# Long convolution and spectral mixing on one core: the last 64 positions of two sequences in one result tile, and the last pair's copies of u on ScalarE

## The chip, the core and the metric

The kernel runs on one core of a Trainium2 chip. The core has TensorE (PE in the profile, its weight loads are PEld), VectorE (DVE), ScalarE (ACT), GpSimd (POOL) and SyncE (SP), which here only issues transfers. Sixteen DMA engines move data between HBM and the on-chip memory SBUF. Matmul results land in PSUM, eight banks of 512 fp32 columns on 128 partitions, from which only DVE and ACT copy here.

The metric is the device time of one execution in microseconds (us). The profile shows one execution instruction by instruction. Its span, from the first to the last instruction, is a little shorter than the time of the same execution.

## What is computed

```python
def _attn_ref(x, h) -> np.ndarray:
    B, S, D = x.shape
    L = 2 * S
    Xf = np.fft.rfft(x, n=L, axis=1)
    Hf = np.fft.rfft(h, n=L, axis=0)
    Yf = Xf * Hf[None, :, :]
    y = np.fft.irfft(Yf, n=L, axis=1)[:, :S, :]
    return y.astype(np.float32)
...
def _moe_ref(x, w_r, w_i, w_ch) -> np.ndarray:
    ...
    X = np.fft.rfft(x, axis=1)
    ...
    Y[:, :n_modes] = Yr + 1j * Yi
    y = np.fft.irfft(Y, n=S, axis=1)
    u = x + y
    return (u + np.maximum(u @ w_ch, 0.0)).astype(np.float32)
```

The input x is 8 sequences of 5696 positions with 128 channels. A long convolution along the positions comes first. Then 64 low modes are mixed across channels, which gives u, and the result is u + relu(u W) at each position, with W of 128x128.

## The kernel before

Everything is worked out as discrete Fourier transforms by matmul, for two sequences at a time: the eight sequences are four pairs, `g_` from 0 to 3, and `b` is the sequence within the pair. Up to about 266 us of the span the spectra of all pairs are made, multiplied by the filter and written to a scratch tensor in HBM. From there on the output phase runs, and all of the change lies in it.

**u tiles.** `u_tile` makes one eighth of u for one sequence: 712 positions, as a 128x712 tile with the channels on the partitions. Its 18 matmuls (two with `IBs` and `C`, sixteen with `S4a` or `S4b` and a spectrum tile `ZT`) fill two PSUM banks. One copy then brings it to SBUF as fp16 in the tensor `UT` (L801, through `evac`, whose line is L311 on ACT and L315 on DVE). A counter decides the engine: of every eight copies five go to ACT and three to DVE (L798). A sequence's u is whole after eight u tiles.

**Result tiles.** `o_tile` makes the results of 512 positions: four matmuls with a slice of `UT` as weights and `WI` (W and the identity, 256 columns) as the moving operand, so that PSUM has u W and u side by side in two banks. ACT makes `R` = relu(u W) (L870), DVE adds u to it (L871) into a buffer `O` or `Os`, and SP sends the buffer to HBM (L320). 5696 positions are 11 such full tiles and 64 positions over; these 64 positions are a twelfth, small tile with one matmul, 64x128 in R and in O, and a transfer of 32 KB. Two full tiles in succession share one `O` buffer and one transfer of 512 KB (the "wide" ones); others have one of 256 KB. There are 7 buffers `O`, 4 buffers `Os`, and 3 buffers `R`.

**Slots.** u tiles and result tiles take PSUM in turn from one ring of four slots of two banks each (`LSLOT`). So the matmuls of a tile wait until the tile four places earlier has been read out: a u tile by its one copy, a result tile by its relu and its add.

**Order.** The order is written out by the loops at L887 to L903, and each engine works through its own list in that order. A list `todo` holds the result tiles still to be made. After each u tile of pair 1 and of pair 2 one or two result tiles of the pair before are taken from it, in turn (24 in all, two sequences with 12 tiles each). In the last pair the u tiles of sequence 0 come first, eight of them, with two result tiles after each; then the eight of sequence 1, with two and three in turn, for which the tiles of the last pair's own sequence 0 have been added to `todo`. The twelve result tiles of the last sequence follow when no u tile is left; this stretch is called the drain here. In the text a step is one u tile with the result tiles that follow it.

The spectrum tiles `ZT` come from the scratch tensor in HBM, in five buffers, by transfers on SP's queue between those of the results.

Of the kernel before, what the change touches and what calls it, by code (L numbers as in the profile page):

```python
# [4 lines left out]
P = 128  # L5
# [118 lines left out]
def bass_long_conv_fft__then__afno_spectral_mix_kernel(nc, x, h, moe_w_r, moe_w_i, moe_w_ch, out):  # L124
    B, S, D = x.shape
# [7 lines left out]
    NP = B // 2  # L133
# [26 lines left out]
    rows = s4.transpose(1, 0, 2, 3).reshape(2 * NK, S)  # L160
# [45 lines left out]
    def at(name, cols, dt, off):  # L206
        return nc.alloc_sbuf_tensor_at(name, [P, cols], dt, offset=off)
# [62 lines left out]
    u_sb = [at(f"UT{i}", S, F16, u_off[i]) for i in range(4)]  # L270
# [21 lines left out]
    def pv(bank, off, dims, p0=0, n=P):  # L292
        return bass.AP(ps, p0 * 4096 + bank * 512 + off, [[4096, n]] + [list(d) for d in dims])
# [5 lines left out]
    def bank(i):  # L299
        return ("bank", i)  # L300
# [3 lines left out]
    def evac(dst, src, reads, writes, scale=None, eng=None, after=()):  # L304
        e = eng
        if e is None:
            turn[0] ^= 1
            e = "scalar" if turn[0] else "vector"
        if e == "scalar":
            if scale is None:  # L310
                R.add(e, lambda h_: h_.copy(dst, src), reads, writes, after=after)  # L311
            else:
                R.add(e, lambda h_: h_.activation(dst, src, COPY, scale=scale), reads, writes, after=after)  # L313
        elif scale is None:
            R.add(e, lambda h_: h_.tensor_copy(dst, src), reads, writes, after=after)  # L315
        else:
            R.add(e, lambda h_: h_.tensor_scalar_mul(dst, src, scale), reads, writes, after=after)  # L317

    def dma(eng, dst, src, ring, reads=(), writes=(), after=()):
        R.add(eng, lambda h_: h_.dma_start(dst, src), reads, writes, ring=ring, after=after)  # L320

    def mm(o, l, r, st, sp, reads, writes):
        R.add("tensor", lambda h_: h_.matmul(o, l, r, start=st, stop=sp), reads, writes)  # L323
# [3 lines left out]
    def once(key, toks):  # L327
        if key in first:
            return []
        first[key] = 1  # L330
        return list(toks)
# [3 lines left out]
    def turns(name, items):  # L335
        i = ring2.get(name, 0)
        ring2[name] = i + 1
        return items[i % len(items)]
# [384 lines left out]
    for g_ in range(NP):  # L723
# [15 lines left out]
        if g_ + 1 < NP:  # L739
            for j in range(6, 32):  # L740
# [3 lines left out]
                if wp and j % 2 == 1:  # L744
                    dst, src_, ring, tok = wp.pop(0)
# [10 lines left out]
    NCH = J // ZB  # L756
    n_ev = [0]
    ahead = {}

    def u_z(i, b, half, alone=False, parts=(0, 1)):  # L760
        g_, c_ = divmod(i, NCH)
        t = ahead.get((i, b, half))
        if t is None:
            t = turns("l", LSLOT)
        z = zt[i % NC]
        for hb in parts:
            if not alone:
                u_c(i, b, half, t, hb, True)
            for pl in range(4):
                for ri in range(2):  # L770
                    pz = half * 8 + hb * 4 + pl
                    so = (c_ * ZB + pz) * NQ
                    n = (P, PB + RB)[ri]
                    mm(pv(t + hb, pl * NQ, [[1, NQ]]), z[ri][0:n, pz * 256 + b * P:pz * 256 + b * P + P], s4_sb[ri][0:n, so:so + NQ],
                       alone and pl == 0 and ri == 0, not alone and pl == 3 and ri == 1, [("zt", i % NC, ri), ("zt0", i % NC), ("s4", ri, 0)] + ([("s4", ri, 1)] if c_ >= NCH // 2 else []), [bank(t + hb)])
        if alone:
            ahead[(i, b, half)] = t
        return t

    def u_c(i, b, half, t, hb, first_):  # L780
        g_, c_ = divmod(i, NCH)
        pl0 = half * 8 + hb * 4
        mm(pv(t + hb, 0, [[1, 4 * NQ]]), c_sb[:, (2 * g_ + b) * P:(2 * g_ + b + 1) * P],
           ib_sb[:, (c_ * ZB + pl0) * NQ:(c_ * ZB + pl0 + 4) * NQ], first_, not first_,
           [("c", g_ // 2), ("ib", 0)] + ([("ib", 1)] if c_ >= NCH // 2 else []), [bank(t + hb)])

    def u_tile(i, b, half):
        g_, c_ = divmod(i, NCH)
        t = ahead.get((i, b, half))
        if t is None:  # L790
            t = u_z(i, b, half)
        else:
            for hb in range(2):
                u_c(i, b, half, t, hb, False)
        ub = (g_ % 2) * 2 + b
        old = {0: WT, 1: WT, 2: U_ALL, 3: U_ALL}[ub]
        n_ev[0] += 1
        e = "scalar" if n_ev[0] % 8 in (0, 2, 3, 5, 7) else "vector"  # L798
        src = pv(t, 0, [[1, NQ], [512, 2], [NQ, 4]])
        evac(bass.AP(u_sb[ub], c_ * ZB + half * 8, [[S, P], [J, NQ], [4, 2], [1, 4]]),  # L800
             src, [bank(t), bank(t + 1)], [("u_", ub, 2 * c_ + half)], eng=e, after=once(("u", ub), old))  # L801
# [36 lines left out]
    NW = S // P  # L838
    TAIL = S - NW * P

    def o_tile(g_, b, r4):
        ub = (g_ % 2) * 2 + b
        bb = 2 * g_ + b
        t = turns("l", LSLOT)
        i = n_o[0]
        n_o[0] += 1
        full = r4 < NW // 4
        last_ = (g_, b) == (NP - 1, 1)
        wide = r4 < (8 if last_ else NW // 4 // 2 * 2)
        big = wide or (last_ and full)  # L850
        h_ = r4 % 2 if wide else 0
        if big:
            if not h_:
                o_cur[0] = turns("o8", list(range(NO8)))
            ob, key, old = o8_sb[o_cur[0]], ("o8", o_cur[0]), o8_old[o_cur[0]]
        else:
            k_ = turns("os", list(range(NO)))
            ob, key, old = o_sb[k_], ("os", k_), o_old[k_]
        OW = 1024 if big else 512
        n, rows = (4, P) if full else (1, TAIL)  # L860
        rd = [("u_", ub, c_) for c_ in range(2 * NCH)] + [("wch",), ("i16",)]
        for j in range(n):
            lh = bass.AP(u_sb[ub], 4 * r4 + j, [[S, P], [NW, P]]) if full else u_sb[ub][:, NW * P:S]
            mm(pv(t + j // 2, (j % 2) * 256, [[1, 256]], 0, rows), lh, WI, True, True, rd, [bank(t + j // 2)])
        bk = [bank(t), bank(t + 1)] if full else [bank(t)]
        rs = r_sb[i % NR]
        rv = bass.AP(rs, 0, [[512, rows], [P, n], [1, P]])
        ov = bass.AP(ob, h_ * 512, [[OW, rows], [P, n], [1, P]])
        src_r, src_u = pv(t, 0, [[256, n], [1, P]], 0, rows), pv(t, P, [[256, n], [1, P]], 0, rows)
        R.add("scalar", lambda e: e.activation(rv, src_r, RELU), bk, [("r", i % NR)], after=once(("r", i % NR), G_ALL + XTT + [("y", 0), ("y", 1), ("id",)]))  # L870
        R.add("vector", lambda e: e.tensor_tensor(ov, src_u, rv, ADD), bk + [("r", i % NR)],  # L871
              [key + (h_,)], after=once(key, old))
        if wide and not h_:
            return
        w_ = (2 if wide else 1) * 4 * D
        if full:
            dst = bass.AP(out.tensor, out.offset + bb * S * D + (4 * r4 - 4 * h_) * D, [[NW * D, P], [1, w_]])
            src = ob[:, 0:w_]
        else:
            dst = bass.AP(out.tensor, out.offset + bb * S * D + NW * P * D, [[D, TAIL], [1, D]])  # L880
            src = ob[0:TAIL, 0:P]
        dma("sync", dst, src, "o", [key + (v_,) for v_ in range(h_ + 1)])

    todo = []
    NB = NCH * NP
    NW4 = NW // 4 + 1
    for g_ in range(NP):  # L887
        last = g_ == NP - 1
        order = [(c_, b) for b in range(2) for c_ in range(NCH)] if last else [(c_, b) for c_ in range(NCH) for b in range(2)]
        for n, (c_, b) in enumerate(order):  # L890
            i = NCH * g_ + c_
            for half in range(2):
                u_tile(i, b, half)
                for _ in range((2, 2 + half)[n >= NCH] if last else 1 + half):
                    if todo:
                        o_tile(*todo.pop(0))
            if b == 1 and i + NC < NB:
                load_zt(i + NC)
            if last and n == NCH - 1:
                todo += [(g_, 0, r4) for r4 in range(NW4)]  # L900
        todo += [(g_, b, r4) for b in range(1 if last else 0, 2) for r4 in range(NW4)]
    while todo:
        o_tile(*todo.pop(0))  # L903
    R.add("sync", lambda e: e.nop(), [], [("o8", i, v_) for i in range(NO8) for v_ in range(2)] + [("os", i, 0) for i in range(NO)])
# [31 lines left out]
```

## Time and profile before

| | |
|---|---|
| time, median of 3 runs | 385.36 us (385.15 to 385.92) |
| the profiled execution: time, span | 385.31 us, 383.2 us |
| busy time in the span: PE, DVE, ACT, POOL | 360.0, 303.1, 310.7, 84.4 us |
| matmuls | 5346 |
| copies of u on ACT, on DVE | 40 of 752 ns mean, 24 of 891 ns median |
| relu R in 128x512, in 64x128 | 88, 8 |
| transfers of results of 32 KB | 8 |

The busy time of an engine is that of its instructions, with overlaps counted once. A line of the timeline gives the start in the span, the length, the engine, the line of the kernel, the tile written and the tile read, shapes, the number of instructions that were merged, and in brackets how long the engine had been idle before and what ended that. "issue" there means that no wait in the profile explains the idle time. Instructions that follow each other at once on ACT and DVE overlap a little: a start can lie before the end of the one before.

### The profile page before, as it was taken

To read this page: it belongs to the slowest core of one execution; us is meant where nothing else is said; L and a number is where in the kernel's file an instruction comes from. 1 tells how busy PE (TensorE), PEld (TensorE's weight loads), DVE (VectorE), ACT (ScalarE), POOL (GpSimd) and SP (SyncE) were. 2 spreads that over 40 slices of the span, in tenths; PEclk is the share of its full clock that TensorE was granted. 3 is DMA by queue.
4 is the path that set the end of the run, shared out by engine and by line. 5 is a ranking of instruction groups with operands and counts; after the bars stand their busy time and mean duration, and the time that the engine had idled before them with its cause. 6 is when DMAs were issued, how large, how long until landed. Compare 5 with 4: busy or idle time off the path is not lost.

```text
span 383.2 us, 12465 instructions
## 1 busy us (share of the span) xinstructions
PE 360.0 (94%) x5346; PEld 277.7 (72%) x5346; DVE 303.1 (79%) x346; ACT 310.7 (81%) x489; POOL 84.4 (22%) x134
## 2 busy tenths in 40 slices
PE   7789899999989999989999899999999999999992
PEld 7778766667856667856657766668898988898871
DVE  3549899988998998989998988766347766777784
ACT  8469689998989997899997899994566776777783
POOL 8703011100733210832212312427000000000000
PEclk9999999999999999999999999998999999999998
DMA  7999959988999995999995899999999999999776
GB/s 140 208 286 362 251 141 240 241 230 240 94 126 202 259 262 167 123 123 246 247 256 129 113 329 347 331 382 399 381 394 359 402 407 417 403 403 361 290 281 275
DMA packets 87201, 103.94 MB, mean 271 GB/s; under 512 B 22883, under 2 KB 72675, under 8 KB 83591
## 3 DMA queue, kind: packets, MB, share of 16 engines
q1 hardware_dynamic: 62667, 67.76, 50.9%
q0 software_dynamic: 24480, 35.40, 43.8%
q8 instruction: 42, 0.69, 0.7%
q14 instruction: 12, 0.10, 0.1%
HBM read 70.61 MB, written 51.12 MB: 318 GB/s over the span
## 4 chain that ended last, share of the span: by engine, by line
PE 73%; DVE 7%; DMA 6%; ACT 6%; issue 3%; POOL 3%; DVEq 0%; POOLq 0%
PE ps L323 73%; DMA Xr<-in_x_dram 4%; DVE As L317 2%; DMA Xt<-in_x_dram 2%; DVE U L630 2%; POOL Xr L320 2%; ACT As L313 2%; ACT R L870 1%; ACT Zs L311 1%; ACT UT L311 1%; POOL Hin L320 1%; DVE Xin L365 1%; DVE Hs L315 1%; ACT Zt L311 1%; ACT Xs L311 1%
## 5 line engine op out<-in xcount | busy, mean ns | idle before, releaser
L638 DVE TENSOR_TENSOR U<-Xs,Hs 128x2048 f16<-128x2048 f16 (+1 forms) x73 | 86.9, 1193 | 13.4 <-ACT Xs L311 12.5
L323 PE MATMUL ps<-U,Wc 128*128 128x512 f16 (+1 forms) x368 | 94.1, 376 | 0.5 <-DVE U L630 0.5
L311 ACT CAST Xs<-ps 128x1024 f16<-128x1024 f32 (+1 forms) x77 | 75.2, 980 | 11.9 <-PE ps L323 6.9
L311 ACT CAST Zs<-ps 128x512 f16<-128x512 f32 (+1 forms) x132 | 69.3, 597 | 1.8 <-PE ps L323 1.8
L871 DVE TENSOR_TENSOR O<-ps,R 128x512 f32<-128x512 f32 x81 | 52.5, 686 | 19.8 <-ACT R L870 12.5
L870 ACT ACTIVATE R<-ps 128x512 f32<-128x512 f32 x96 | 50.9, 573 | 14.3 <-PE ps L323 13.9
L317 DVE TENSOR_SCALAR As<-ps 128x720 f16<-128x720 f32 x70 | 57.7, 886 | 5.2 <-PE ps L323 4.6
L323 PE MATMUL ps<-F,Xin 128*128 128x180 f16 x512 | 53.7, 249 | 3.8 <-DVE Xin L365 2.5
L323 PE MATMUL ps<-As,M 64*128 64x128 f16 x1440 | 50.3, 217 | 3.5 <-DVE U L630 2.9
L323 PEld LDWEIGHTS ps<-F,Xin 128*128 128x128 f16 x512 | 44.4, 155 | 12.6 <-DVE As L317 2.8
L323 PE MATMUL ps<-WI,UT 128*128 128x256 f16 x360 | 51.8, 278 | 0.5 <-DVE O L871 0.4
L313 ACT ACTIVATE As<-ps 128x720 f16<-128x720 f32 (+1 forms) x61 | 45.7, 769 | 7.9 <-PE ps L323 6.4
L323 PEld LDWEIGHTS ps<-U,Wc 128*128 128x128 f16 x368 | 28.6, 97 | 29.4 <-ACT Zs L311 3.7
L323 PEld LDWEIGHTS ps<-As,M 64*128 64x128 f16 x1440 | 40.6, 94 | 9.7 <-DVE U L630 3.6
L311 ACT CAST UT<-ps 128x712 f16<-128x712 f32 x40 | 30.0, 752 | 18.0 <-PE ps L323 17.0
L323 PEld LDWEIGHTS ps<-WI,UT 128*128 128x128 f16 x360 | 39.3, 152 | 4.2 <-issue 1.9
L323 PE MATMUL ps<-IBs,C 128*128 128x356 f16 x128 | 39.9, 321 | 0.6
L320 POOL DMA_DIRECT2D Xt<-in_x_dram x40 | 21.4, 540 | 80.3 <-PE ps L323 79.8
L323 PEld LDWEIGHTS ps<-G,Zs 128*128 128x128 f16 x512 | 26.1, 96 | 14.5 <-ACT Zs L311 2.0
L638 DVE TENSOR_TENSOR U<-ps,Hs 128x2048 f16<-128x2048 f32 x15 | 34.3, 2285 | 0.0
L323 PE MATMUL ps<-G,Zs 128*128 128x128 f16 (+2 forms) x512 | 32.3, 192 | 0.1
L311 ACT CAST Zt<-ps 128x512 f16<-128x512 f32 x52 | 28.6, 627 | 0.3 <-PE ps L323 0.3
(88 smaller groups left out, 502.1 us busy)
## 6 DMA issues: line engine op xcount, KB each, us to landing
out_dram<-O SPq DMA_DIRECT2D x39, 512.0 KB, 7.8
zscr<-Zs SPq DMA_DIRECT2D x62, 256.0 KB, 6.8
zscr<-Zt SPq DMA_DIRECT2D x26, 256.0 KB, 6.2
Xt<-in_x_dram POOLq DMA_DIRECT2D x20, 320.0 KB, 7.2
W<-wscr POOLq DMA_DIRECT2D x4, 1024.0 KB, 6.7
M<-cM POOLq DMA_DIRECT2D x5, 720.0 KB, 17.6
ZT0a<-zscr SPq DMA_DIRECT2D x3, 1024.0 KB, 9.0
Hs<-Hs SPq DMA_DIRECT2D x44, 64.0 KB, 6.0
```

What stands on the lines that cost most here:

```text
L311: R.add(e, lambda h_: h_.copy(dst, src), reads, writes, after=after)
L313: R.add(e, lambda h_: h_.activation(dst, src, COPY, scale=scale), reads, writes, after=after)
L315: R.add(e, lambda h_: h_.tensor_copy(dst, src), reads, writes, after=after)
L317: R.add(e, lambda h_: h_.tensor_scalar_mul(dst, src, scale), reads, writes, after=after)
L320: R.add(eng, lambda h_: h_.dma_start(dst, src), reads, writes, ring=ring, after=after)
L323: R.add("tensor", lambda h_: h_.matmul(o, l, r, start=st, stop=sp), reads, writes)
L365: R.add("vector", lambda e: e.tensor_copy(bass.AP(x_sb, i * XN * XS, [[XW, NQ], [XS, XN], [1, D]]), src), list(toks) + XZ, [("xin", i)])
L630: R.add("vector", lambda e, b=b, s_=s_: e.tensor_tensor(bass.AP(u_s[i], b * 512, [[2048, P], [1024, 2], [1, n * D]]), s_, hv, MULT), [tok, ...
L638: R.add("vector", lambda e: e.tensor_tensor(uv, src, hv, MULT), bk + [("h", t, 0), ("h", t, 1, 0), ("h", t, 1, J)], [("u", i)])
L870: R.add("scalar", lambda e: e.activation(rv, src_r, RELU), bk, [("r", i % NR)], after=once(("r", i % NR), G_ALL + XTT + [("y", 0), ("y", 1 ...
L871: R.add("vector", lambda e: e.tensor_tensor(ov, src_u, rv, ADD), bk + [("r", i % NR)], [key + (h_,)], after=once(key, old))
```

## The change

The two sequences of a pair now share one tile for their last 64 positions. Each pair's tile has two matmuls, one from each sequence's `UT`, side by side in one bank, one relu and one add of 64x256, and one transfer of 64 KB that writes to both sequences. It is put at the end of the pair's list; in the last pair it stands between the full tiles of sequence 0 and those of sequence 1, since it needs u of both. In the last pair all sixteen copies of u go to ACT.

```diff
-        e = "scalar" if n_ev[0] % 8 in (0, 2, 3, 5, 7) else "vector"
+        e = "scalar" if n_ev[0] % 8 in (0, 2, 3, 5, 7) or g_ == NP - 1 else "vector"
...
+        ubs = [ub] if full else [ub, ub + 1]
...
-        n, rows = (4, P) if full else (1, TAIL)
-        rd = [("u_", ub, c_) for c_ in range(2 * NCH)] + [("wch",), ("i16",)]
+        n, rows = (4, P) if full else (2, TAIL)
+        rd = [("u_", v_, c_) for v_ in ubs for c_ in range(2 * NCH)] + [("wch",), ("i16",)]
         for j in range(n):
-            lh = bass.AP(u_sb[ub], 4 * r4 + j, [[S, P], [NW, P]]) if full else u_sb[ub][:, NW * P:S]
+            lh = bass.AP(u_sb[ub], 4 * r4 + j, [[S, P], [NW, P]]) if full else u_sb[ubs[j]][:, NW * P:S]
...
-            dst = bass.AP(out.tensor, out.offset + bb * S * D + NW * P * D, [[D, TAIL], [1, D]])
-            src = ob[0:TAIL, 0:P]
+            dst = bass.AP(out.tensor, out.offset + bb * S * D + NW * P * D, [[D, TAIL], [S * D, 2], [1, D]])
+            src = bass.AP(ob, 0, [[OW, TAIL], [D, 2], [1, D]])
...
-    NW4 = NW // 4 + 1
+    NW4 = NW // 4
...
             if last and n == NCH - 1:
                 todo += [(g_, 0, r4) for r4 in range(NW4)]
+        todo += [(g_, 0, NW4)] * last
         todo += [(g_, b, r4) for b in range(1 if last else 0, 2) for r4 in range(NW4)]
+        todo += [(g_, 0, NW4)] * (not last)
```

## The prediction

> **What bounds the kernel now.** I read the page first, then the table of stretches for the output phase, then the timelines of PE's weight loads, of ACT, DVE and SP, engine by engine.
>
> ```profile
> PE 360.0 (94%) x5346; PEld 277.7 (72%) x5346; DVE 303.1 (79%) x346; ACT 310.7 (81%) x489; POOL 84.4 (22%) x134
> PE 73%; DVE 7%; DMA 6%; ACT 6%; issue 3%; POOL 3%; DVEq 0%; POOLq 0%
> ```
>
> ```profile
> core 0: us, PE busy (x) PEld busy (x) DVE busy (x) ACT busy (x) POOL busy (x), PEclk, DMA share, GB/s
> 315.00:330.00 15.00, 14.77 (x211) 13.04 (x209) 10.85 (x18) 10.53 (x20) 0.00 (x0) 1.00 1.02 414
> ...
> 368.00:378.00 10.00, 7.57 (x53) 5.49 (x51) 9.01 (x16) 8.23 (x16) 0.00 (x0) 1.00 0.82 325
> 378.00:383.20 5.20, 0.00 (x0) 0.00 (x0) 0.00 (x0) 0.00 (x0) 0.00 (x0) 0.77 0.52 197
> ```
>
> The chain is 73% PE. At 315 to 330 us DVE and ACT have over a quarter of their time free, and PE's weight loads fill 13 of 15 us: PE sets the pace, and what it loses it loses in gaps. From 368 on DVE is busy 9.01 of 10 us: the drain is DVE's. After 378 only transfers are left.
>
> The gaps are found on PE's weight loads:
>
> ```profile
> 293.59 0.44 PEld L323 LDWEIGHTS ps<-WI,UT 128*128 128x128 f16 x4
> 294.19 0.11 PEld L323 LDWEIGHTS ps<-WI,UT 128*64 128x64 f16 x1 [0.16 <-issue]
> 294.55 0.10 PEld L323 LDWEIGHTS ps<-IBs,C 128*128 128x128 f16 x1 [0.26 <-issue]
> ...
> 300.33 0.87 PEld L323 LDWEIGHTS ps<-WI,UT 128*128 128x128 f16 x8
> 301.24 0.10 PEld L323 LDWEIGHTS ps<-IBs,C 128*128 128x128 f16 x1
> ...
> 308.11 0.10 PEld L323 LDWEIGHTS ps<-IBs,C 128*128 128x128 f16 x1 [0.26 <-issue]
> ...
> 334.98 0.11 PEld L323 LDWEIGHTS ps<-WI,UT 128*64 128x64 f16 x1 [0.16 <-issue]
> 335.34 0.10 PEld L323 LDWEIGHTS ps<-IBs,C 128*128 128x128 f16 x1 [0.25 <-issue]
> ```
>
> A step with two full tiles goes into the next u tile without a gap (0.87 us of loads, next load 0.91 us after the first). A step with a full and a small tile waits 0.16 us before and 0.26 us after the small one. The small tile gives PE 0.11 us of work, but takes a slot for a relu and an add like any other, so the ring of four slots turns faster than it is emptied.
>
> **The change, part by part.** The program itself gives the order after: PE keeps 5346 matmuls; eight small tiles become four double ones.
>
> *1. Pairs 1 and 2 (about 282 to 335 us).* Per pair two small tiles go, each 0.11 us of matmul and 0.42 us of gap: 1.06 us. One double tile comes, with 2 x 0.11 = 0.22 us of matmul. It stands alone in the last step of the pair, followed by a u tile of 0.98 us (two halves of 281.61 - 281.12 = 0.49, below), so the ring has time and I give it no gap. The full tiles that move up beside another full tile cost their 0.44 us wherever they stand. The saving is 1.06 - 0.22 = 0.84 us at most; two-tile and one-tile steps show stray gaps of up to 0.1 us (at 301.24: 0.04), so I take 0.75, and 1.5 us for two pairs. Bounds: all gaps stay away, -1.7; each double tile keeps a longer gap, -0.3 (below, a rival).
>
> ```profile
> 281.12 0.10 PEld L323 LDWEIGHTS ps<-IBs,C 128*128 128x128 f16 x1
> 281.61 0.10 PEld L323 LDWEIGHTS ps<-IBs,C 128*128 128x128 f16 x1
> ```
>
> *2. The last pair's u tiles (335.34 to 366.60, where the last one starts).* Between them stand 33 result tiles before and after: 31 full and 2 small ones, then 32 full and a double one. Here six copies move from DVE to ACT, which by the durations adds 6 x 0.752 = 4.5 us to ACT and takes 6 x 0.889 = 5.3 us from DVE. What counts is the chain from the start of a u tile to the release of the last result tile behind it, which the u tile after next needs.
>
> ```profile
> 347.03 0.10 PEld L323 LDWEIGHTS ps<-IBs,C 128*128 128x128 f16 x1 [0.28 <-issue]
> 350.99 0.10 PEld L323 LDWEIGHTS ps<-IBs,C 128*128 128x128 f16 x1 [0.16 <-ACT UT L311]
> 352.87 0.10 PEld L323 LDWEIGHTS ps<-IBs,C 128*128 128x128 f16 x1
> 357.42 0.10 PEld L323 LDWEIGHTS ps<-IBs,C 128*128 128x128 f16 x1 [0.16 <-ACT UT L311]
> 361.85 0.10 PEld L323 LDWEIGHTS ps<-IBs,C 128*128 128x128 f16 x1
> 366.60 0.10 PEld L323 LDWEIGHTS ps<-IBs,C 128*128 128x128 f16 x1
> ```
>
> ```profile
> 348.24 0.75 ACT L311 CAST UT<-ps 128x712 f16<-128x712 f32 x1 [0.74 <-PE ps L323]
> 348.89 1.09 ACT L870 ACTIVATE R<-ps 128x512 f32<-128x512 f32 x2
> ...
> 354.73 1.58 ACT L870 ACTIVATE R<-ps 128x512 f32<-128x512 f32 x3
> ```
>
> ```profile
> 349.58 1.29 DVE L871 TENSOR_TENSOR O<-ps,R 128x512 f32<-128x512 f32 x2 [1.07 <-PE ps L323]
> ...
> 363.80 0.89 DVE L315 CAST UT<-ps 128x712 f16<-128x712 f32 x1
> ```
>
> With the copy on ACT: u tile at 347.03, copy 348.24, relus 348.89 (0.65 later), adds 349.58 to 350.87, next use of the slot 350.99: 3.96 us for two steps, where PE's loads alone would fill 2 x 0.98 + 2 x 0.87 = 3.70. The profile names an ACT copy as releaser, but this one had ended at 348.99; it is the add that ended last. All eight steps of sequence 0 on ACT cost 4 x 3.96 = 15.84 us; now they take 350.99 - 335.34 = 15.65. That is +0.2. For sequence 1 every second step has three result tiles. From one such step to the next it is 4.55 us with the copy on ACT (352.87 to 357.42), and 4.43 (with a small tile in it) and 4.75 us with the copy on DVE (to 361.85 and 366.60), since DVE does the copy of 363.80 ahead of three adds. After: 3 x 4.55 = 13.65 against 13.73 now: -0.1. The step between, 1.88 now, follows from the slower rhythm: +0.1. Together +0.2 us. Bounds: the least of these numbers everywhere (3.70 and 4.43) -1.3; the largest (4.75 for sequence 1, and the same excess of 0.2 over 4.55 on each 3.96) +1.5. Is ACT able to? Back to back a relu takes 0.49 ((1.58 - 0.60) / 2) and a copy 0.65, so a pair of steps with five relus costs ACT 2 x 0.65 + 5 x 0.49 = 3.75 of 4.55 us.
>
> *3. The drain.* After the last copy of u (367.82) DVE has two full tiles and a small one to add before the last eleven, and a small one behind them:
>
> ```profile
> 367.82 0.75 ACT L311 CAST UT<-ps 128x712 f16<-128x712 f32 x1
> 368.47 1.24 ACT L870 ACTIVATE R<-ps 128x512 f32<-128x512 f32 x3
> ```
>
> ```profile
> 369.18 0.69 DVE L871 TENSOR_TENSOR O<-ps,R 128x512 f32<-128x512 f32 x1 [0.60 <-ACT R L870]
> 369.79 0.87 DVE L871 TENSOR_TENSOR Os<-ps,R 128x512 f32<-128x512 f32 x2
> 370.68 6.80 DVE L871 TENSOR_TENSOR O<-ps,R 128x512 f32<-128x512 f32 x11
> 377.39 0.27 DVE L871 TENSOR_TENSOR Os<-ps,R 64x128 f32<-64x128 f32 x1
> ```
>
> After, only one full tile and the double one stand ahead: one full tile has moved into the u steps, among the 33 tiles of part 2. Gone ahead of the eleven: an add of 0.61 (369.18 to 369.79) and one of 0.27. Added: the double tile's add, between 0.27 (64x128) and 0.69 us (128x512), by columns 0.27 + 0.42 / 3 = 0.41. So -0.47; bounds -0.6 to -0.2. The eleven keep (6.80 - 0.69) / 10 = 0.61 us each, DVE's own pace.
>
> *4. The end.* The last small tile's transfer goes:
>
> ```profile
> 377.90 0.55 SPq L320 DMA_DIRECT2D out_dram<-O  x1
> 378.50 0.66 SPq L320 DMA_DIRECT2D out_dram<-Os  x1
> ```
>
> ```profile
> out_dram<-O SPq DMA_DIRECT2D x3, 256.0 KB, 5.1
> out_dram<-Os SPq DMA_DIRECT2D x4, 32.0 KB, 3.9
> 381.50:382.00 0.50, 0.00 (x0) 0.00 (x0) 0.00 (x0) 0.00 (x0) 0.00 (x0) 0.50 0.07 29
> ```
>
> The last 256 KB, issued at 377.90, land near 383.0, as late as the small one (378.50 + 3.9 = 382.4). So its going is worth 0 to 0.6; I take 0.1. At 381.5 the share is 0.07, about one engine of sixteen still at work.
>
> The other transfers change little: eight of 32 KB become four of 64 KB with the same rows of 512 bytes, on SP's queue, which waits for DVE between issues anyway. The double tile waits for two sequences' `UT`; both are whole a step or more before it, except in the drain, where it waits for the copy at 367.82 just as the eleven do.
>
> Sum: -1.5 + 0.2 - 0.5 - 0.1 = -1.9 us on the profiled 385.31 us, that is 383.4. The median of the runs, 385.36, is 0.05 above that execution, so the same holds for it.
>
> **The rivals.**
>
> *The merged tile keeps the bubble.* The gaps come from how long a slot is held, and the double tile holds it longer (relu and add 0.27 to 0.4 us each). If each of the two double tiles of pairs 1 and 2 shows both gaps and the 0.25 us on top, 0.67 us, part 1 shrinks from 1.7 to 0.3, and the time is 385.31 - 0.3 + 0.2 - 0.6 = 384.6. For it: nothing but the ring. Against it: the tile stands alone in its step. The Trainium skill (Perfetto Trace Analysis, Optimizing Scalar/DVE Operations) has a rule on this side: where these engines are not saturated but cause bubbles on others, smaller instructions may let work finish sooner; by it the merge is the wrong direction. The rows above have the bubble at the smallest tile of all, so I side with them.
>
> *The transfers bound pairs 0 to 2.* The DMA share is 1.02 at 315 to 330 us.
>
> ```profile
> DMA to landing us min/median/max: 2.6/7.2/12.0
> ```
>
> Results land up to 12.0 us after their issue. Seven `O` buffers last seven transfers of 512 KB, five of which fall in 13.56 us (294.55 to 308.11): 19.0 us, less some 2.5 for filling one. So 16 us are allowed, 4 more than used; the 1.5 us gained eat into this but don't use it up, and neither DVE nor PE waits for a transfer there now. If they did, part 1 would be lost: 385.31 + 0.2 - 0.6 = 384.9.
>
> *ACT becomes the bound in the last pair (slower).* If copies and relus don't overlap in the new mix, ACT pays 0.75 for a copy and 0.60 for a relu. A two-tile step is then 0.75 + 1.20 + 0.23 (from the end of the matmuls, 347.03 + 0.98, to the copy at 348.24) = 2.2 instead of 1.98, a pair of steps with five relus 1.50 + 3.0 + 0.46 = 5.0 instead of 4.55: 8 x 0.2 + 3.5 x 0.45 = +3.2, so 386.6. It decides from the point where five relus and two copies need more than 4.55 us. Against it: 348.24 and 354.73 show the overlap in just this order. The same section of the Trainium skill would move work to ScalarE where VectorE is saturated; DVE at 10.85 of 15 us isn't, so the rule gives the move no support.
>
> *The end is shorter still.* The lone engine that works until 382 has fallen behind by something that may not fall together with the drain again (a 16 KB instruction transfer is in that stretch):
>
> ```profile
> q8 instruction: 1, 0.02, 7.2%
> ```
>
> Without it the end comes 1.5 us sooner: 381.9.
>
> **How the numbers follow.** Forecast 383.4, chance 0.57, with an own range of 382.6 to 384.4 (part 1 and part 2 each off by half a microsecond). Shorter end 0.13; bubble kept 0.09; transfers bound 0.09; ACT bound 0.12. About 0.2% (0.77 us) is what a measurement of this kernel can tell from no change, so faster means below 384.6. Forecast and shorter end lie there, and the kept bubble on the edge: 0.57 + 0.13 + half of 0.09, less 0.02 for the forecast's upper edge, is 0.73. Same: transfers bound 0.09, the other half and the edge: 0.15. Slower: 0.12. The range from 382.2 to 385.6 leaves out the slower case and half of the shorter end.
>
> **What would show it.** Right: no gap around the double tiles at about 308 and 334 us; the first u tile of the last pair near 333.8 instead of 335.34; all its copies on ACT, steps of 3.96 and 4.55; the last add ending near 375.7 instead of 377.5; the end 5.6 us behind it. Wrong: gaps of 0.4 us at the double tiles; DVE or PE waiting for transfers; ACT busy without a break in the last pair while PE waits for copies of u, with three-tile steps at 5 us.

## The result and the profile after

| | before | after |
|---|---|---|
| time, median of 22 runs each | 385.69 us (383.69 to 389.45) | 383.14 us (381.96 to 387.21) |
| ratio of the times, 95% interval | | 0.9927 (0.9903 to 0.9951) |
| profiled execution: time, span | 385.31, 383.2 us | 387.21, 385.1 us |

The change is worth 2.6 us between the medians (1.9 to 3.7 by the interval). The forecast, 383.4 us, holds, but two of its four terms are not what was forecast.

The profiled execution of after is the longest of its 22 runs, longer than that of before. Much of the reason is in the chain of waits, in order of time (start, length, what it was):

```profile
247.86 13.02 DMA zscr<-Zs
...
260.96 0.60 ACT Zs L311
```

ScalarE's idle time before `Zs`, grouped by line for 250 to 268 us, ends on this transfer:

```profile
L311 ACT CAST Zs<-ps 128x512 f16<-128x512 f32 (+1 forms) x10 | 5.0, 565 | 3.8 <-DMA zscr<-Zs 3.8
```

This wait of 3.8 us lies ahead of the output phase, in code that the change leaves alone. Of the runs below, copies_only (2.6 us) and before_shifted (1.8 us), which have the old tails, show it too, and the second profile of after (after_again) does not. So the two spans can't be subtracted; the two output phases can, both counted from their first relu R. On ScalarE's timeline of before that is

```profile
282.80 0.60 ACT L870 ACTIVATE R<-ps 128x512 f32<-128x512 f32 x1 [0.69 <-PE ps L323]
```

and on that of after, with the relu of the second double tile and the last copy of u:

```profile
288.06 0.60 ACT L871 ACTIVATE R<-ps 128x512 f32<-128x512 f32 x1 [0.69 <-PE ps L323]
...
339.84 0.38 ACT L871 ACTIVATE R<-ps 64x256 f32<-64x256 f32 x1
...
372.02 0.75 ACT L311 CAST UT<-ps 128x712 f16<-128x712 f32 x1 [0.51 <-PE ps L323]
```

From there to the end of the span before took 383.2 - 282.80 = 100.40 us, after 385.1 - 288.06 = 97.04: 3.36 us less. The output phase of after begins 5.26 us later; 3.8 us of that is the wait above, the rest also arose ahead of it and was not followed up. PE's weight loads of after:

```profile
298.85 0.88 PEld L323 LDWEIGHTS ps<-WI,UT 128*128 128x128 f16 x8
299.81 0.10 PEld L323 LDWEIGHTS ps<-IBs,C 128*128 128x128 f16 x1
...
311.38 0.10 PEld L323 LDWEIGHTS ps<-IBs,C 128*128 128x128 f16 x1
...
312.52 0.14 PEld L323 LDWEIGHTS ps<-WI,UT 128*64 128x64 f16 x2
312.85 0.10 PEld L323 LDWEIGHTS ps<-IBs,C 128*128 128x128 f16 x1 [0.20 <-issue]
...
339.42 0.10 PEld L323 LDWEIGHTS ps<-IBs,C 128*128 128x128 f16 x1 [0.20 <-issue]
...
347.31 0.10 PEld L323 LDWEIGHTS ps<-IBs,C 128*128 128x128 f16 x1 [0.16 <-ACT UT L311]
...
351.27 0.10 PEld L323 LDWEIGHTS ps<-IBs,C 128*128 128x128 f16 x1 [0.16 <-ACT UT L311]
...
357.12 0.10 PEld L323 LDWEIGHTS ps<-IBs,C 128*128 128x128 f16 x1
...
361.24 0.14 PEld L323 LDWEIGHTS ps<-WI,UT 128*64 128x64 f16 x2 [0.16 <-issue]
361.69 0.10 PEld L323 LDWEIGHTS ps<-IBs,C 128*128 128x128 f16 x1 [0.31 <-ACT UT L311]
...
366.24 0.10 PEld L323 LDWEIGHTS ps<-IBs,C 128*128 128x128 f16 x1 [0.16 <-issue]
...
370.81 0.10 PEld L323 LDWEIGHTS ps<-IBs,C 128*128 128x128 f16 x1 [0.16 <-issue]
```

The double tile isn't free of a gap: 0.20 us behind it at 312.85 and at 339.42. The step with it takes 1.47 us (311.38 to 312.85), for 0.98 us of a u tile and 0.14 us of loads. Where the first small tile of a pair was, a full one now stands (the second half of the loads at 298.85), and this brings nothing: from the first relu to the next u tile it is 11.75 us in both kernels (282.80 to 294.55, 288.06 to 299.81). What the first pair saves comes after that: to the end of its last step it is 13.56 us before (294.55 to 308.11) and 13.04 after (299.81 to 312.85). The last pair's u tiles begin at 339.42, and the last of them at 370.81. The drain on VectorE:

```profile
373.36 1.01 DVE L872 TENSOR_TENSOR Os<-ps,R 128x512 f32<-128x512 f32 x2 [0.97 <-PE ps L323]
374.55 6.67 DVE L872 TENSOR_TENSOR O<-ps,R 128x512 f32<-128x512 f32 x11 [0.18 <-issue]
```

The group of 1.01 us holds one full tile's add and the double one's. The last add ends at 374.55 + 6.67 = 381.22. What follows is transfers, by the issues of 364 to 386 us (issuer, count, size, median us to landing) and the table of stretches (last columns: granted PE clock, DMA share, GB/s):

```profile
out_dram<-O SPq DMA_DIRECT2D x3, 256.0 KB, 3.4
...
out_dram<-Os SPq DMA_DIRECT2D x1, 64.0 KB, 3.4
```

```profile
383.50:384.00 0.50, 0.00 (x0) 0.00 (x0) 0.00 (x0) 0.00 (x0) 0.00 (x0) 0.50 0.39 143
384.00:384.50 0.50, 0.00 (x0) 0.00 (x0) 0.00 (x0) 0.00 (x0) 0.00 (x0) 0.50 0.03 12
```

The same table of before:

```profile
381.00:381.50 0.50, 0.00 (x0) 0.00 (x0) 0.00 (x0) 0.00 (x0) 0.00 (x0) 0.50 0.06 25
...
382.00:382.50 0.50, 0.00 (x0) 0.00 (x0) 0.00 (x0) 0.00 (x0) 0.00 (x0) 0.50 0.05 16
```

Before, one engine of sixteen (share 0.06) worked on alone for 1.5 us; after, the engines stop almost together. The end, from the last full add to the end of the span, is 385.1 - 381.22 = 3.88 us; before it was 383.2 - 377.48 = 5.72. The last 256 KB land 3.4 instead of 5.1 us behind their issue. So the account, after against before:

| stretch of the output phase | before | after | difference | forecast |
|---|---|---|---|---|
| first relu to first u tile of the last pair | 52.54 | 51.36 | -1.18 | -1.5 |
| that to the last u tile | 31.26 | 31.39 | +0.13 | +0.2 |
| that to the end of the last full add | 10.88 | 10.41 | -0.47 | -0.47 |
| that to the end of the span | 5.72 | 3.88 | -1.84 | -0.1 |
| sum | 100.40 | 97.04 | -3.36 | -1.9 |

### The profile page after: what moved, and what is told of

Read it like the earlier page. It is cut to its first block, busy times and chain, and to the rows that moved or that the text cites. A ratio compares the mean times of both kernels' runs of the same rounds, so it can differ in the third digit from the quotient of the medians.

```text
span 385.1 us, 12438 instructions
## 1 busy us (share of the span) xinstructions
PE 362.4 (94%) x5346; PEld 280.7 (73%) x5346; DVE 296.6 (77%) x336; ACT 314.3 (82%) x491; POOL 85.2 (22%) x134
## 4 chain that ended last, share of the span: by engine, by line
PE 76%; DMA 8%; DVE 6%; ACT 4%; POOL 3%; issue 2%; DVEq 0%; ACTq 0%; POOLq 0%
PE ps L323 76%; DMA Xr<-in_x_dram 4%; DMA zscr<-Zs 3%; DVE As L317 2%; DVE U L630 2%; POOL Xr L320 2%; ACT As L313 2%; ACT R L871 1%; POOL Hin L320 1%; DVE Xin L365 1%; DVE Hs L315 1%; ACT Zt L311 1%; ACT Zs L311 0%; DMA Hs<-Hs 0%; ACT Xs L311 0%
## 5 line engine op out<-in xcount | busy, mean ns | idle before, releaser
L872 DVE TENSOR_TENSOR O<-ps,R 128x512 f32<-128x512 f32 x81 | 52.3, 685 | 20.1 <-ACT R L871 11.2
L871 ACT ACTIVATE R<-ps 128x512 f32<-128x512 f32 (+1 forms) x92 | 50.5, 591 | 8.5 <-PE ps L323 8.4
L311 ACT CAST UT<-ps 128x712 f16<-128x712 f32 x46 | 34.5, 752 | 19.2 <-PE ps L323 18.0
```

## The experiments

Every experiment was profiled, and the four stretches can be read in each, whatever came ahead of them. The fifth and sixth columns are the last 16 KB instruction transfer of the trace: its start, counted from the start of the last copy of u, and its length. The last full add ends 9.2 us behind that copy with the merged tails (8.87 in tail_last) and 9.65 with the old ones.

```
                 to u0   u0-u15  to last add   end    transfer  length   output phase
before           52.54   31.26   10.88         5.72   +5.46     1.74     100.40
before_again     52.23   31.27   10.87         5.65   +5.36     1.69     100.02
copies_only      52.51   31.14   10.86         5.54   +3.11     1.89     100.05
before_shifted   52.03   31.28   10.86         3.61   +0.53     0.95      97.78
after            51.36   31.39   10.41         3.88   +0.71     0.96      97.04
after_again      51.38   31.41   10.41         3.42   +1.07     1.39      96.62
merge_only       51.36   31.09   10.43         3.79   +1.40     1.48      96.67
tail_last        51.37   31.39   10.08         4.22   -0.17     1.91      97.06
rhythm           51.35   31.41   10.41         3.65   -0.19     1.62      96.82
after_shifted    51.58   31.38   10.42         4.13   +4.30     0.96      97.51
warm_60          51.37   31.42   10.42         4.87   +6.32     0.95      98.08
warm_76          51.27   31.38   10.41         5.57   +7.31     1.90      98.63
no_tails         50.64   31.44   10.42         3.39   +0.58     1.25      95.89
```

The same kernel differs by up to 0.3 us in the first column (before and before_again) and 0.5 in the end (after and after_again).

**One half of the change at a time.** merge_only has the double tiles, but the old choice of engines:

```diff
-        e = "scalar" if n_ev[0] % 8 in (0, 2, 3, 5, 7) or g_ == NP - 1 else "vector"
+        e = "scalar" if n_ev[0] % 8 in (0, 2, 3, 5, 7) else "vector"
```

> The merged tiles alone, the copies of u in the last pair shared out as before. Theory M (the merge is the gain, the copies are about neutral): pairs 1 and 2 shorter by 1.2 us (first relu to the last pair's first u tile 51.4 instead of 52.5 us), the u steps of the last pair within 0.5 us of before, the drain 0.3 shorter; with the end as before -1.3 us (ratio 0.9965), with an end 1.8 us shorter -3.1 us (0.992). Rival C (relieving DVE is the gain, the merge does nothing): ratio 1.000. Rival E (the end is shorter because no small transfer is last): last full add to the end of the span 3.9 us here as in the changed kernel.

copies_only is the kernel before with the other half, the same line as changed:

```diff
-        e = "scalar" if n_ev[0] % 8 in (0, 2, 3, 5, 7) else "vector"
+        e = "scalar" if n_ev[0] % 8 in (0, 2, 3, 5, 7) or g_ == NP - 1 else "vector"
```

> The last pair's copies of u all on ACT, the small tiles as before. Theory M: the small tiles keep 0.4 us of gaps each, pairs 1 and 2 as before, the last pair's u steps 0.2 us longer to 0.2 shorter, with 4.55 us from one three-tile step to the next; ratio 0.999 to 1.001. Rival C: -2 us or more, ratio 0.995 or below. Rival E: the end stays at 5.7 us.

Beside them both kernels ran unchanged.

> The kernel before, once more, as a second profile of it and as the size of chance. All theories: ratio 1.000 with its interval around it. If the end of 5.7 us (last full add to the end of the span) belongs to the order of the program, it is 5.7 again, with a 16 KB instruction transfer in the drain and one engine at work alone at the very end; if it is chance, it is shorter.

> The changed kernel once more. All theories: ratio 0.993 and no wait of 3.7 us at 257 us, which the change cannot have made. Theory M: first relu to the end of the span 97 us as in its first profile, against 100.4 before; end 3.9 us again if it belongs to the order of the program.

Measured against before: merge_only 0.9946 (0.9909 to 0.9984), copies_only 0.9994 (0.9963 to 1.0025), before_again 0.9996 (0.9971 to 1.0022), after_again 0.9905 (0.9873 to 0.9937). The copies alone bring nothing that the times show; the merge brings a gain by itself. The interval of merge_only overlaps that of after_again, so by the times alone the copies might still help once the tails are merged. The stretches speak against that: the last pair's u tiles take 31.09 us with mixed copies and 31.39 with all of them on ScalarE, so here the move costs 0.3 us, and the rest of merge_only's output phase is that of after. In copies_only PE's weight loads still show the gaps around each small tile:

```profile
312.56 0.11 PEld L323 LDWEIGHTS ps<-WI,UT 128*64 128x64 f16 x1 [0.16 <-issue]
312.93 0.10 PEld L323 LDWEIGHTS ps<-IBs,C 128*128 128x128 f16 x1 [0.26 <-issue]
```

The surprise is the end: 5.54 us in copies_only, 3.79 in merge_only. With the merge an instruction transfer also moved, from 3.1 us behind the last copy of u or later to 1.4 or earlier. Hence the next experiments.

The long end of copies_only does not look like that of before, though. In its table of stretches hardly any DMA engine is at work from 377.5 to 378.5 us, right behind the instruction transfer (375.62 to 377.51), and the sixteen engines are late as a whole instead, until some 386.2 us, 4 us behind the last full add:

```profile
377.50:378.00 0.50, 0.50 (x5) 0.42 (x4) 0.50 (x2) 0.45 (x2) 0.00 (x0) 1.00 0.03 8
378.00:378.50 0.50, 0.50 (x6) 0.41 (x4) 0.50 (x2) 0.50 (x2) 0.00 (x0) 1.00 0.06 25
...
386.00:386.50 0.50, 0.00 (x0) 0.00 (x0) 0.00 (x0) 0.00 (x0) 0.00 (x0) 0.50 0.32 95
386.50:387.00 0.50, 0.00 (x0) 0.00 (x0) 0.00 (x0) 0.00 (x0) 0.00 (x0) 0.50 0.05 16
```

On SP's timeline the two issues of `Os` from 375.18 on take 2.73 us (1.05 in before), and the next result is issued only at 377.95. Whether the transfer held them up was not tested.

**Moving the instruction transfer.** The kernel starts with `WARM` = 92 matmuls whose results are not used. Their number shifts all later PE instructions, and nothing else in the program.

```diff
-    WARM = 92
+    WARM = 116
```

in the kernel before (before_shifted), and 68 in the changed one (after_shifted):

> The kernel before with 24 more of the idle matmuls at its very start (48 more PE instructions), which moves all later 16 KB instruction transfers of PE by 48 instructions, a sixth of a block, towards an earlier place in the program. Theory M (one engine is late at the end because a 16 KB instruction transfer falls among the last results): the last such transfer lands near the last copy of u instead of 5.4 us behind it, and the last full add to the end of the span is 3.8 us instead of 5.7; ratio about 0.995. Rival E (the small last transfer makes the end long): 5.7 us, ratio 1.000. If the transfer is not PE's, it doesn't move, and the end stays too.

> The changed kernel with 24 fewer idle matmuls at its start (48 fewer PE instructions), the opposite shift. Theory M: the last 16 KB instruction transfer falls later, among the last results (3 to 6 us behind the last copy of u), and the end grows from 3.4 to 3.9 to about 5.5 us; against the kernel before the ratio is 0.996 to 0.998 instead of 0.9905 to 0.993. Rival E: end 3.8 us as before the shift.

before_shifted took 384.97 us, ratio 0.9973 (0.9939 to 1.0006): not settled by the time. Its profile is clear. The table of stretches:

```profile
384.00:384.50 0.50, 0.00 (x0) 0.00 (x0) 0.00 (x0) 0.00 (x0) 0.00 (x0) 0.50 1.02 370
384.50:385.10 0.60, 0.00 (x0) 0.00 (x0) 0.00 (x0) 0.00 (x0) 0.00 (x0) 0.50 0.18 47
385.10:385.60 0.50, 0.00 (x0) 0.00 (x0) 0.00 (x0) 0.00 (x0) 0.00 (x0) 0.50 0.00 0
```

All sixteen engines work to 384.5 and stop within 0.6 us. The transfer stands in 371.5 to 373.5 us, by the DMA queues of that window (count, MB, share), before the last results are queued:

```profile
q8 instruction: 1, 0.02, 3.0%
```

The kernel before, tails and all, thus ends 3.61 us behind its last full add instead of 5.72. after_shifted put the transfer at +4.3 as meant, yet its end is 4.13, short of the 5.5 expected and no longer than the ends of the kernels with an early transfer (3.39 to 4.22); its time, 389.26 us (1.007, 1.0035 to 1.0104), is longer by what lies ahead of the output phase. In the table of stretches of after_shifted the clock is 0.83 from 10 to 20 us and PE busy 6.70 us,

```profile
10.00:20.00 10.00, 6.70 (x65) 6.69 (x66) 5.38 (x7) 4.31 (x6) 7.07 (x11) 0.83 1.05 207
```

where after has 1.00 and 9.26 us:

```profile
10.00:20.00 10.00, 9.26 (x116) 8.83 (x114) 6.62 (x8) 5.42 (x8) 7.74 (x11) 1.00 1.05 207
```

So it stayed open whether the merged tail itself made the end short. Two more counts, 76 and 60, were to tell:

> The changed kernel with 76 instead of 92 matmuls at the start, 32 PE instructions fewer: the transfer should stand at about 3.0 us behind the last copy of u, where the kernel before with the last pair's copies on ScalarE had it (3.1 us, and an end of 5.5 us behind the last full add). Theory T: an end of 4.5 to 5.5 us here. Theory F: 3.6 to 4.3 us.

> The changed kernel with 60 instead of 92 matmuls at the start, 64 PE instructions fewer. With 68 the last 16 KB instruction transfer moved from 0.7 us to 4.3 us behind the last copy of u; with 60 it should stand at about 5.4 us, where the kernel before had it. Theory T (the transfer among the last results makes the end long wherever the results are queued deep): the end behind the last full add is 5 to 5.7 us, as in the kernel before. Theory F (the changed tails themselves keep the end short: the transfer counts only if it is slow, 1.7 us, and behind the merged tail it is not): the end stays at 3.6 to 4.3 us with the transfer at 5.4.

In neither did the transfer land where it was expected (+7.31 instead of +3.0 with 76, +6.32 instead of 5.4 with 60); where it falls was not worked out right by counting instructions. But both put it among the last results, and both ends grew, to 5.57 and 4.87 us. warm_76, the DMA queues of 377 to 379 us and the table of stretches:

```profile
q8 instruction: 1, 0.02, 5.9%
```

```profile
381.00:382.00 1.00, 0.00 (x0) 0.00 (x0) 0.00 (x0) 0.00 (x0) 0.00 (x0) 0.50 1.02 393
382.00:382.50 0.50, 0.00 (x0) 0.00 (x0) 0.00 (x0) 0.00 (x0) 0.00 (x0) 0.50 0.85 328
382.50:383.00 0.50, 0.00 (x0) 0.00 (x0) 0.00 (x0) 0.00 (x0) 0.00 (x0) 0.50 0.07 25
...
384.00:384.50 0.50, 0.00 (x0) 0.00 (x0) 0.00 (x0) 0.00 (x0) 0.00 (x0) 0.50 0.04 16
```

The lone engine is back, for nearly 2 us, with the changed tails. In warm_60 the share is 0.06 from 383.5 to 384.5 us and 0.03 in the half microsecond after. That the merged tail keeps the end short by itself is refuted. The single times of these two (387.24 and 387.71 us, one run each) say little beside that.

**The last small transfer.** tail_last puts the last pair's double tile at the very end, where the small one of before stood:

```diff
-        todo += [(g_, 0, NW4)] * last
         todo += [(g_, b, r4) for b in range(1 if last else 0, 2) for r4 in range(NW4)]
-        todo += [(g_, 0, NW4)] * (not last)
+        todo += [(g_, 0, NW4)]
```

> The changed kernel with the last pair's double tile behind the eleven full tiles instead of ahead of them, so that a small transfer is the last again. Theory M: the last full add comes 0.3 to 0.4 us sooner, the double tile's add behind it; the time within 0.3 us of the changed kernel. Rival E: the end is 5.7 us again behind the last full add, the time 1.5 us longer than the changed kernel's.

Measured: 384.32 us, 0.9976 (0.9942 to 1.001). VectorE's timeline:

```profile
371.11 6.67 DVE L872 TENSOR_TENSOR O<-ps,R 128x512 f32<-128x512 f32 x11 [0.15 <-ACT R L871]
377.69 0.41 DVE L872 TENSOR_TENSOR Os<-ps,R 64x256 f32<-64x256 f32 x1
```

The eleven adds start 0.33 us sooner behind the last u tile and the end takes 4.22 instead of 3.88: what one stretch gives the other takes. With a small transfer last the end is not 5.5 us, so the small transfer was not the cause of the long one. The output phase is 97.06 us, as after. The time was expected within 0.3 us of after's and its median is 1.2 us longer; the intervals of the two ratios overlap, and the difference does not lie in the output phase.

**The rhythm of pairs 0 to 2.** The first theory of the short part 1 was that the ScalarE copy in a two-tile step holds the ring up. rhythm gives ScalarE the copies of the one-tile steps and VectorE those of the two-tile steps:

```diff
-        e = "scalar" if n_ev[0] % 8 in (0, 2, 3, 5, 7) or g_ == NP - 1 else "vector"
+        e = "scalar" if half == 0 or g_ == NP - 1 else "vector"
```

> The changed kernel, but in pairs 0 to 2 DVE copies u in the steps with two result tiles and ACT in those with one (eight and eight instead of six and ten). Theory L (what part 1 of the prediction lacked is a slot chain of 3.37 us for two steps through an ACT copy in a two-tile step, where PE needs 3.33): with DVE there the chain is 3.1, the two-tile steps go from 1.92 to 1.88 us, and first relu to the last pair's first copy falls from 52.6 by 0.5 to 0.9 us. If the lack lies elsewhere (transfers, chance), it stays at 52.5; if DVE is overloaded by this (2.6 of 3.3 us), it grows.

Measured: 382.42 us, 0.9909 (0.9879 to 0.9939), and 51.35 us to the last pair's first u tile, as after: the theory as stated fell. The timelines of PE's loads, of ScalarE and of VectorE show a chain of the same length elsewhere:

```profile
298.86 0.10 PEld L323 LDWEIGHTS ps<-IBs,C 128*128 128x128 f16 x1
...
302.22 0.10 PEld L323 LDWEIGHTS ps<-IBs,C 128*128 128x128 f16 x1
```

```profile
300.07 0.75 ACT L311 CAST UT<-ps 128x712 f16<-128x712 f32 x1 [0.37 <-PE ps L323]
300.72 0.60 ACT L871 ACTIVATE R<-ps 128x512 f32<-128x512 f32 x1
```

```profile
301.41 0.69 DVE L872 TENSOR_TENSOR O<-ps,R 128x512 f32<-128x512 f32 x1 [0.66 <-issue]
```

Now the chain runs through the one-tile step: u tile 298.86, copy 300.07, relu 300.72, add 301.41 to 302.10, next such u tile 302.22. That is 3.36 us for a pair of steps, hardly above what PE's loads alone fill (2 x 0.98 + 0.44 + 0.87 = 3.27).

**The price of the double tile.** no_tails drops this line from the changed kernel:

```diff
-        todo += [(g_, 0, NW4)] * (not last)
```

> The changed kernel without the double tile of pairs 0 to 2: the last 64 positions of the first six sequences are not written. It prices the double tile. In the profile of the changed kernel the step with it takes 1.43 us against 1.00 us for a u tile alone, twice between the first relu R and the first copy of u of the last pair, and the two-tile steps have risen to 1.91 to 2.00 us from 1.88 to 1.93. Theory P (the double tile itself costs its 0.43 us and nothing else): that stretch, 52.57 us in the mean of the kernels with merged tiles, falls to 51.7, two times 0.43 less. Theory Q (the double tile also gives the ring time to catch up, so part of it comes back in the steps behind): it falls to 51.9 to 52.3. Theory S (the double tile makes the steps behind it late as well, which is why they rose): it falls below 51.5. The time goes down by the same, 382.3 by P; the rest of the output phase does not change (u tiles of the last pair 31.4, drain 9.2).

Between the first relu and the last pair's first copy of u it took 51.86 us instead of 52.57, 0.36 us for each double tile; the account by u tiles above, 50.64 against 51.38 in the mean, gives 0.37. The step without the tile runs without a gap on PE's weight loads,

```profile
309.35 0.10 PEld L323 LDWEIGHTS ps<-IBs,C 128*128 128x128 f16 x1
...
310.35 0.10 PEld L323 LDWEIGHTS ps<-IBs,C 128*128 128x128 f16 x1
...
311.34 0.44 PEld L323 LDWEIGHTS ps<-WI,UT 128*128 128x128 f16 x4
...
323.00 0.10 PEld L323 LDWEIGHTS ps<-S4b,ZT4b 84*128 84x128 f16 x1 [0.24 <-issue]
```

two u tiles of 1.00 us in a row. The 51.86 us lie 0.16 above the first theory's figure and just below the range of the second. The last row explains the difference: a u tile of this one profile has a stray gap, and its two-tile step takes 2.11 us (321.83 to 323.94) where the same step of after takes 1.96 (324.30 to 326.26). Without these 0.15 us it would be 51.71, the first theory's figure: the double tile costs 0.43 us, and that the ring makes up a part of it is not shown. It does not make the steps behind it late. The ratio of the times, 0.9867 (0.9802 to 0.9932), is that of less work.

## Why the prediction was right, point by point

The number was hit in part by luck. Part 1 gave 0.3 to 0.55 us less than forecast and the end 1.7 us more, so the output phase gained 3.36 us (3.40 between the second profiles), not 1.9. The forecast also started from a median of 385.36 us, where 22 runs gave 385.69. What happened is, by its mechanism, the rival of the shorter end, which had 381.9 us.

**1. Pairs 1 and 2: the merge saves, but by another account, and over-sized.** Forecast -1.5 us; the two profiles give -1.18, and the means of four profiles with the old tails (52.33) and eight with the merged ones (51.38) give -0.95. Most of the difference between these two is one stray gap in before, inside a u tile:

```profile
320.75 0.10 PEld L323 LDWEIGHTS ps<-S4a,ZT4a 128*128 128x128 f16 x1 [0.37 <-issue]
```

Two steps of the sum failed. The first is that full tiles that move up "cost their 0.44 us wherever they stand" while a small one costs 0.53: a full tile in the small one's turn takes just as long. The 11.75 us in both kernels show it for pair 1; in pair 2 the half with its first small tile takes 13.42 us in before_again (309.86 to 323.28) and 13.41 in after_again (307.89 to 321.30). So the going of a pair's first small tile saves nothing, and the saving lies in the pair's last step, which had a full and a small tile (2.00 us, 306.11 to 308.11) and now has the double tile alone (1.47). The second is that the double tile "stands alone" and so has no gap, the first of the signs that were named for being right: it has one (0.20 us behind it), and it costs 0.36 to 0.43 us instead of 0.22 for its matmuls and about 0.1 of stray gaps. From 52.33 to 50.64 with no tails at all, the four small tiles cost 1.69 us, 0.42 each on average. The rival in which the bubble is kept was thus half right: the double tile keeps a gap and costs about what one small tile did. Its price was too high, though; it left 0.3 us of gain where 0.95 to 1.18 were measured.

The Trainium skill (Perfetto Trace Analysis, Optimizing Scalar/DVE Operations), whose rule of smaller instructions was that rival's, does not fit these runs: merging alone gave 0.9946 (0.9909 to 0.9984).

**2. The last pair's u tiles: right.** +0.13 measured, +0.2 forecast (+0.3 against merge_only, which differs in the copies alone). Steps of sequence 0 go by 3.96 us for two (347.31 to 351.27) as foreseen, and from one three-tile step to the next it is 4.57 us (357.12 to 361.69), foreseen 4.55. ScalarE did not become the bound; the rows name its copy of u as releaser again, with gaps of 0.16 us, as before. The double tile has gaps of 0.16 and 0.31 us around it there (361.24, 361.69), but its pair of steps takes 4.57 us where the next, with a full tile in its place, takes 4.55 (361.69 to 366.24), which fits a chain over the slots that bounds both.

**3. The drain: right.** -0.47 from the last u tile to the last full add. That it agrees to the hundredth is chance, for it came differently by parts: the first of the eleven adds is 0.34 us earlier behind the last u tile (366.60 to 370.68 before, 370.81 to 374.55 after, with a gap of 0.18 that was not there), and the eleven themselves take 6.67 instead of 6.80 us. The double add takes what was interpolated, 0.41 us, by the groups of 280 to 386 us:

```profile
L872 DVE TENSOR_TENSOR O<-ps,R 128x512 f32<-128x512 f32 x81 | 52.3, 685 | 20.1 <-ACT R L871 11.2 <-PE ps L323 5.8 <-issue 3.1
...
L872 DVE TENSOR_TENSOR Os<-ps,R 64x256 f32<-64x256 f32 x4 | 1.6, 411 | 1.1 <-ACT R L871 1.1
```

These rows also answer the rival of the transfers: ScalarE, PE and "issue" account for all of the 20.1 us, so no full add waited for a buffer that a transfer still held. Nor did PE wait for a transfer between 288 and 371 us.

**4. The end: wrong.** Forecast -0.1 us, measured -1.84. The step priced only the going of the last small transfer, and that was right to be small: tail_last, which has one again, ends at 4.22. What decided is the rival that had a chance of 0.13: an instruction transfer no longer falls among the last results. before_shifted shows it without the change (5.72 to 3.61), warm_76 and warm_60 with the change (3.88 to 5.57 and 4.87). So most of the 1.84 us goes with where that transfer falls, not with the smaller number of tiles; after_shifted, whose end stayed at 4.13, shows that a late place alone is not enough.

What stays open: why the transfer moved between the two kernels, though both have 5346 matmuls, and why a count of 76, 68 or 60 places it where it does. Nor is the size of the delay settled. With the transfer at +5.4 us or later (before, before_again, warm_60, warm_76) one engine is alone for about 1.5 us or more, whether the transfer took 0.95 or 1.9 us; at +3.1 and +4.3 (copies_only, after_shifted) it is alone at the end for about half a microsecond. So how late the transfer comes seems to count for more than its length. This is read off six profiles, not tested by itself, and copies_only has its long end in another way.

## What to carry to other kernels

Where tiles of unequal size share a ring of buffers, a tile's price is its turn in the ring: 0.42 us on average for a small tile with 0.11 us of matmul, about as much (0.36 to 0.43) for two of them in one turn. So the gap beside a small tile is not what its going saves: where a full tile moved into its turn nothing was saved (11.75 us in both kernels), and the gain came at the end of the list, where a turn fell away. Before a change at the end of a kernel is credited or blamed for the last microseconds, look whether one of the DMA engines works on alone, and shift the instruction stream by some instructions in both kernels: here that alone moved the end by some 2 us, more than the 1.5 us (1.18 + 0.47 - 0.13) that the change saved ahead of it.

## What was not expected of the hardware

**Instruction transfers and results share engines.** In the four profiles where a 16 KB instruction transfer starts 5.4 us or more behind the last copy of u, one DMA engine (share 0.06, 25 GB/s) is at work for 1.5 to 2 us after the fifteen others are done. The trace does not name the engines; that the late one is the one that carried the transfer is inferred. That the transfer belongs to PE's instructions is inferred: only the number of PE's first matmuls was changed, and the transfer moved with it. The Trainium skill (Runtime: NRT & Kernel Launch, Instruction fetch mechanics) says that the sequencer fetches its instructions by its own DMA queue in blocks of 16 KiB and that the cost of crossing a boundary is mostly hidden. The size agrees with the rows (0.02 MB each); the compute engines don't show the cost (the last full add is 10.41 us behind the last u tile in warm_76 as in after), and it falls on the results instead: 5.57 against 3.88 us at the end.

**Fewer matmuls at the start, a lower clock behind them.** With 68 instead of 92 of them the granted clock was 0.83 from 10 to 20 us, and PE was busy 6.70 instead of 9.26 us there. With 60 the clock was 0.83 there too; with 76 it was 1.00, but 0.92 from 20 to 30 us. These are one profile each. after_shifted, with 68, took 389.26 us in 12 runs, 6 us more than after.
